# Opening of a fused attention and gated-MLP block: left-over Q/K rows on SyncE's queue, one more buffer for a transposed chunk, half of a chunk's statistics on ScalarE, long output columns first

## The chip, the cores and the metric

The kernel runs on one core of a Trainium2 chip. A core has five engines, each with its own instruction stream: TensorE (PE, matrix products; its weight loads are shown apart as PEld), VectorE (DVE), ScalarE (ACT), GpSimd (POOL) and SyncE (SP), which here only issues DMA transfers. Transfers are issued from the streams of SP, ACT and POOL and run on 16 DMA engines. The metric is the device time of one execution in microseconds; lower is better. Before the change it is 565.48 us (median of three runs, 563.97 to 566.1).

## What is computed

S = 2048 rows of D = 576 columns pass through an attention part (A) and a gated MLP part (B). Each is preceded by a layer norm, whose result is scaled and shifted by columns computed from a condition vector c, and followed by a gated residual. Attention has 32 heads of 18 columns and looks at 8 positions back, 2 apart. The MLP multiplies two projections to F = 4608 columns (no non-linear function) and projects back.

```
mod = (silu(c) @ w_mod)            # six rows of D: sa, ca, ga, sb, cb, gb
h = layernorm(x) * (1 + ca) + sa
q, k, v = split(h @ wqkv)          # 32 heads of 18
logits[s, w] = q[s] . k[s - 2 w] * 18 ** -0.5,  w = 0..7, masked where s - 2 w < 0
x = x + ga * (sum_w softmax(logits)[s, w] v[s - 2 w]) @ wo
h = layernorm(x) * (1 + cb) + sb
x = x + gb * ((h @ w_gate) * (h @ w_up)) @ w_down
```

All inputs and the output are bfloat16.

## The kernel before

The rows are cut into 8 chunks of 256 (`CH`), each of two halves of 128 (`ST` = 2, index j). D = 576 is handled as `KT` = 5 blocks of 128, the last with 64 rows only (kt = 4, the "left-over" rows of a weight). The order of the instructions of each engine is the order in which the program writes them; no scheduler moves them. What is emitted on one engine, or on one engine's DMA queue, runs in that order.

The program has an opening and then five groups of row tiles (`GROUPS`), each with a stage `gate_up` (36 steps f; 18 matmuls a step into the banks `pg` and `pu`, copies by ACT at L678 and L679, a product on DVE at L683) and a stage `down` (products with `w_down` into `acc` and `accr`). The attention of later chunks runs as pieces spread between the steps of these stages. The weight blocks `wgu` of `gate_up` (four steps each) come over SP's queue; in the first group blocks 0 to 4 are loaded ahead, and block 5 is issued when the matmuls of block 0 are done.

The opening handles chunk 0's attention whole, chunk 1's up to Q, K and V, and the same for chunk 2. Its loads go out in the order of the program: on SP's queue x of chunk 0, the blocks of `wmA` (the part of `w_mod` for sa and ca, kt = 0 to 3), the Q/K weights `wqk` for kt = 0, 1, then x of chunk 1 (`load_x(1)`), kt = 2, 3, then the value weights `wv`, x of chunk 2, `wmB`, `wo`, `wmC` (the ga part), and the first weights of the MLP. The left-over rows of `wqk` (kt = 4) are issued from ACT's stream, behind the third block of `wmA` (`behind(load_qk(nc.scalar, KF), wmA_in[2])`, L801).

The steps of the opening that the change and the prediction speak of:

- Columns of the modulation (`pm_part`, L824): matmuls with `wmA`, with idle matmuls (`run_idle`, L190) between the parts.
- Q and K of chunk 0 (`qk0`, L866): groups of nine matmuls, one group for each half j and each block kt, in the order (0, kt 0), (0, kt 1), (1, kt 0), (0, kt 4), (1, kt 1), (0, kt 2), (1, kt 4), (0, kt 3), (1, kt 2), (1, kt 3): `QKK` = (0, 1, 4, 2, 3). One of the nine reads `wq4`, columns of `wqk` that POOL copies together for each kt (L815). `qk0_out` copies the sums out of PSUM (L872 to L875).
- Logits of chunk 0: products on DVE (`pj`, L892), sums on PE (`lj`, L900), maximum and Exp (`max_j`, L906 to L908), sum and weights (`sum_j`, L914 to L916).
- Chunk i, i > 0: statistics (`a_ln`, L257 to L259: two BATCH_NORM_STATS2 and one aggregate for each half, on DVE), 1/sqrt by Ln and Exp on ACT (L262, L263), normalising on DVE (L267), transposes on PE and modulation into `hT` (`a_t`: L296, then L283 on DVE and L285 on ACT), Q and K (`a_q`, five calls, L374, copies by ACT at L377 to L382), V (`a_v`, L397 to L402). `hT` comes from the pool `hTp` with one buffer; chunk 0's comes from the pool `vshp` with two buffers, which otherwise holds the gathered values `vsh`.
- For chunk 2 the transposes of the two halves stand apart: `between` puts the second part of the ga row (`mod_row`, L321) and `to_keys` (L514, L517, copies L520) between them.
- `av_mul` (DVE, L529) and `av_sum` (PE, L540): values of chunk 0 times weights, and their sum; `b_wj` (L554): the product with `wo` for chunk 0.

In `down`, `b_o` transposes the attention output of a chunk (L502) and copies it to `oT` in two copies (L503: blocks 0 to 3 at once; L504: block 4); `b_w(i, j)` multiplies it with `wo`, first the last 64 columns (L569), then the first 512 (L571), and adds the residual on DVE (L573 to L575).

Of the kernel before, what the change touches and what calls it, by code (L numbers as in the profile page):

```python
# [7 lines left out]
BF = mybir.dt.bfloat16  # L8
F32 = mybir.dt.float32
# [9 lines left out]
P = 128  # L19
# [26 lines left out]
def kernel(  # L46
# [47 lines left out]
    def js(j):  # L94
        return slice(j * P, (j + 1) * P)
# [76 lines left out]
    def behind(dma, load):  # L172
        tc.add_manual_dep(dma.ins, load.ins.name, SYNC, reason="value rows go first")
# [13 lines left out]
    def run_idle(n):  # L187
        idle = ps([P, P], F32, "idle")
        for _ in range(n):
            nc.tensor.matmul(idle[:], lhsT=zero[:], rhs=zero[:], start=True, stop=True, skip_group_check=True)  # L190
# [23 lines left out]
    def load_wmA(eng, kt):  # L214
        p, r = rows(kt)
        return eng.dma_start(wmA[p, kt, :, :].rearrange("p b n -> p (b n)"), w_mod[r, 0:2 * D])

    def load_qk(eng, kt):
        p, r = rows(kt)
        return eng.dma_start(wqk[p, kt, :], A_wqkv[r, 0:2 * D])  # L220

    wmA_in = [load_wmA(nc.sync, kt) for kt in range(KF)]
    for kt in range(KF):
        if kt == 2:
            load_x(1)
        load_qk(nc.sync, kt)
# [22 lines left out]
    def ln_parts(src, tag):  # L249
        stats = small.tile([P, ST, 2, 6], F32, name="ln_stats" + tag)  # L250
        mv = small.tile([P, ST, 2], F32, name="ln_mv" + tag)
        rstd = small.tile([P, ST], F32, name="ln_rstd" + tag)
        xn = lnp.tile([P, ST, DP], BF, name="ln_xn")

        def stat(j, hfs=(0, 1)):
            for hf in hfs:
                nc.vector.bn_stats(stats[:, j, hf, :], src(j)[:, hf * 288:(hf + 1) * 288])  # L257
            if hfs[-1] == 1:
                nc.vector.bn_aggr(mv[:, j, :], stats[:, j, :, :].rearrange("p a b -> p (a b)"))  # L259

        def rsq(r):
            nc.scalar.activation(rstd[:, r], mv[:, r, 1], ACTF.Ln, bias=eps[:])  # L262
            nc.scalar.activation(rstd[:, r], rstd[:, r], ACTF.Exp, scale=-0.5)  # L263

        def norm(j):
            for d0, s0, n in ((0, 0, D), (D, D - 64, 64)):
                nc.vector.tensor_scalar(xn[:, j, d0:d0 + n], src(j)[:, s0:s0 + n], mv[:, j, 0:1], rstd[:, j:j + 1],  # L267
                                        ALU.subtract, ALU.mult)
        return xn, stat, rsq, norm

    def layernorm(src, tag):
        xn, stat, rsq, norm = ln_parts(src, tag)
        for j in range(ST):
            stat(j)

        def norms(js=range(ST)):
            for j in js:
                norm(j)
        return xn, lambda: rsq(slice(0, ST)), norms

    def modulate(dst, s, m, vi_scale, vi_shift, on_dve):
        if on_dve:
# [52 lines left out]
    def a_ln(i):  # L335
        x = x_in.pop(i)
        xn, rsq, norm = layernorm(lambda j: x[:, j, :], "a")
        aa[i] = dict(xn=xn, rsq=rsq, norm=norm)
# [3 lines left out]
        aa[i]["norm"]()  # L342

    def a_tiles(i):
        hT = hTp.tile([P, KT, CH], BF, name="hT") if i else vshp.tile([P, KT, CH], BF, name="vsh")
        aa[i].update(hT=hT, qT=qTs[i % 2], kT=kTs[i % 2])

    def a_halo(i):
# [6 lines left out]
    def a_t(i, on_dve=(0, 1, 2), between=None):  # L355
        a_tiles(i)
        hT = aa[i]["hT"]
        transposed(aa[i]["xn"], lambda m: hT[:, m, :], (0, 1), 0, between)(on_dve)
# [25 lines left out]
    def a_q(i, g):  # L384
        qk_tiles(i, QGRP[g], slice(0, CH), nc.scalar.copy)
        if g == 2:
            a_halo(i)
# [107 lines left out]
    def b_o(i):  # L495
        o = o_sbs[i % 2]
        pA = ps([P, 4, CH], BF, "oT_pA")
        pB = ps([P, 1, CH], BF, "oT_pB")
        for m in range(KT):
            d = pA[:, m, :] if m < 4 else pB[:, 0, :]  # L500
            for j in range(ST):
                nc.tensor.transpose(d[:, js(j)], o[:, j, m * P:(m + 1) * P], ident[:])  # L502
        nc.scalar.copy(oT[:, 0:4, :], pA[:])  # L503
        nc.scalar.copy(oT[:, 4, :], pB[:, 0, :])  # L504

    keyed = []
# [1 line left out]
    def to_keys(j):  # L508
        pk = ps([P, W, H], F32, "pk")
        for w in range(W):  # L510
            sh = DIL * (W - 1 - w)
            at = attn0[:, w // 4, :, w % 4, :]
            cross = j == 0 and sh > 0
            nc.tensor.matmul(pk[:, w, :], lhsT=slide[:, P + sh:2 * P + sh], rhs=at[:, j, :], start=True, stop=not cross,  # L514
                             skip_group_check=True)
            if cross:
                nc.tensor.matmul(pk[:, w, :], lhsT=slide[:, sh:P + sh], rhs=at[:, 1, :], start=False, stop=True,  # L517
                                 skip_group_check=True)
        kt = lgp.tile([P, W, H], BF, name="keyed", tag="lgs")
        nc.scalar.copy(kt[:], pk[:])  # L520
        keyed.append(kt)
# [43 lines left out]
    def b_w(i, j):  # L565
        pw = ps([P, 512], F32, "pw")
        pwr = ps([P, 64], F32, "pwr")
        for m in range(KT):
            nc.tensor.matmul(pwr[:], lhsT=oT[:, m, js(j)], rhs=wo[:, m, 512:D], start=(m == 0), stop=(m == KT - 1))  # L569
        for m in range(KT):  # L570
            nc.tensor.matmul(pw[:], lhsT=oT[:, m, js(j)], rhs=wo[:, m, 0:512], start=(m == 0), stop=(m == KT - 1))  # L571
        xt = x1p.tile([P, D], BF, name="x1")
        nc.vector.tensor_tensor(xt[:, 512:D], pwr[:], ga_bc[:, 512:D], ALU.mult)  # L573
        nc.vector.tensor_tensor(xt[:, 0:512], pw[:], ga_bc[:, 0:512], ALU.mult)
        nc.vector.tensor_tensor(xt[:], xt[:], x_res[i][:, j, :], ALU.add)  # L575
        x1.setdefault(i, []).append(xt)

# [220 lines left out]
    nc.vector.tensor_tensor(sc_w[:], wide(c_col), wide(e_f), ALU.mult)  # L798
    stat0(1)
    rsq0(slice(1, 2))  # L800
    behind(load_qk(nc.scalar, KF), wmA_in[2])  # L801
    for j in range(ST):
        norm0(j)
    nc.vector.tensor_copy(sc[:], sc_w[:, :, 0])
# [32 lines left out]
    t0(1)  # L837
    run_idle(2)
    pm_part(MODK[3])
    run_idle(8)  # L840
    pm_part(MODK[4])
    run_idle(5)

# [45 lines left out]
    def pj(j, w):  # L889
        off = HALO - DIL * (W - 1 - w) + j * P  # L890
        prods[j, w] = prodp.tile([P, KT, P], BF, name="prodj", tag="prod")
        nc.vector.tensor_tensor(prods[j, w][:], aa[0]["qT"][:, :, js(j)], aa[0]["kT"][:, :, off:off + P], ALU.mult)  # L892
# [53 lines left out]
        lj(0, w)  # L946
    for w in range(6, 8):
        pj(0, w)
    a_q(1, 0)
    for w in range(6, 8):  # L950
        lj(0, w)
# [12 lines left out]
    a_q(1, 3)  # L964
    for w in range(4, 6):
        lj(1, w)
    a_ln(2)
    aa[2]["rsq"]()
    a_q(1, 4)
    for w in range(6, 8):  # L970
        lj(1, w)
    max_j(1)
    mod_columns(wmB, 1)
    aa[2]["norm"]((0,))
    sum_j(1)
    aa[2]["norm"]((1,))
    a_v(1, 0)
    ga_row = lambda part: mod_row(lambda p, k: wmC[p, k, :] if k < KF else wmCr[p, :], ga_bc, sc_bc, (part,))
    ga_out = [ga_row((0, 512))]

    def between():
        ga_out.append(ga_row((512, D)))
        for j in range(ST):
            to_keys(j)

    a_t(2, (0, 1, 2), between)
    a_v(1, 1)
    av_mul(0, 0)
    av_mul(0, 1)
# [106 lines left out]
```

## Time and profile before

| | us |
|---|---|
| median of three runs (lowest, highest) | 565.48 (563.97, 566.1) |
| the profiled execution, time | 564.62 |
| its span, first to last instruction | 562.9 |
| PE busy in the span | 548.8 |
| DVE busy | 330.7 |
| ACT busy | 248.4 |
| start of the first `gate_up` matmul (L654) | 54.47 |
| start of the first product with `w_down` (L721) | 94.91 |

All times of single instructions are microseconds from the start of the span. A row of the timeline gives the start, the duration, the engine, the line, the operation, the tiles written and read with their shape, how many equal instructions are merged, and in brackets how long the engine stood idle before and what released it; a q behind the engine's name marks its instruction queue, which issues DMA transfers. A row of the windows view gives the stretch and its length, the busy time (and number of instructions) of PE, PEld, DVE, ACT and POOL, the granted clock of PE (1.00 is full speed), the mean busy share of the DMA engines, and GB/s.

Of the page, the costliest groups are the matmuls of the MLP:

```profile
L654 PE MATMUL pg<-h2T,wgu 64*128 64x512 bf16 (+2 forms) x1440 | 277.3, 333 | 0.0
L654 PE MATMUL pu<-h2T,wgu 64*128 64x512 bf16 (+2 forms) x1440 | 276.0, 333 | 0.0
...
L721 PE MATMUL acc<-wd,hh 128*128 128x512 bf16 (+1 forms) x556 | 140.2, 369 | 0.2
```

The columns behind the bar are the busy time, the mean duration in ns, and the idle time of the engine just before these instructions: the MLP's matmuls follow each other without a pause.

### The profile page before, as it was taken

The numbers are of one execution on the slowest core, as the hardware profiler recorded it, in microseconds if no ns is written. First come the engines' busy times: TensorE is split into PE (matmuls) and PEld (weight loads), VectorE is DVE, ScalarE is ACT, GpSimd is POOL, SyncE is SP. The second block draws the span as 40 slices with busy tenths as digits, with TensorE's granted clock in tenths as the row PEclk, the third lists the DMA queues.
The fourth block names the chain that finished last, engine by engine and source line by source line (L and its number), as shares of the span: only waits on it lengthen the run. The fifth ranks groups of instructions, "written<-read, shape, count | busy, mean of one in ns | idle before, by whom it ended". The sixth has DMA issues, their size and how long they took to land.

```text
span 562.9 us, 14324 instructions
## 1 busy us (share of the span) xinstructions
PE 548.8 (97%) x6021; PEld 328.1 (58%) x6059; DVE 330.7 (59%) x799; ACT 248.4 (44%) x572; POOL 66.8 (12%) x104
## 2 busy tenths in 40 slices
PE   6999999999999999999999999999999999999997
PEld 5777887666444445656444444665555555565564
DVE  7688889995767787251867787406727614322202
ACT  2545566244555653323355654231466611455500
POOL 5101301213000001111200100111100022000020
PEclk9899999999999999999999999999999999999999
DMA  8999999754844854332854765333856565655053
GB/s 276 263 269 262 322 295 355 246 168 116 297 137 163 281 156 141 94 108 89 280 172 148 227 211 169 108 106 125 300 189 201 188 201 170 191 181 196 1 170 115
DMA packets 69994, 108.14 MB, mean 192 GB/s; under 512 B 3658, under 2 KB 57754, under 8 KB 69930
## 3 DMA queue, kind: packets, MB, share of 16 engines
q1 hardware_dynamic: 58592, 61.13, 35.3%
q0 software_dynamic: 11168, 45.81, 25.4%
q8 instruction: 47, 0.77, 0.6%
q10 hardware_dynamic: 170, 0.30, 0.2%
q14 instruction: 17, 0.14, 0.1%
HBM read 102.78 MB, written 4.44 MB: 190 GB/s over the span
## 4 chain that ended last, share of the span: by engine, by line
PE 88%; DVE 1%; issue 1%; ACT 1%; ACTq 0%
PE pg L654 28%; PE pu L654 22%; PE acc L721 20%; PE pq L374 4%; PE accr L725 4%; PE pw L571 3%; PE pv L397 2%; PE lg L432 2%; PE tr_pA L296 1%; PE oT_pA L502 1%; PE tr_pB L296 1%; PE pwr L569 0%; DVE o_t L760 0%; PE lt L448 0%; PE pvr L399 0%
## 5 line engine op out<-in xcount | busy, mean ns | idle before, releaser
L654 PE MATMUL pg<-h2T,wgu 64*128 64x512 bf16 (+2 forms) x1440 | 277.3, 333 | 0.0
L654 PE MATMUL pu<-h2T,wgu 64*128 64x512 bf16 (+2 forms) x1440 | 276.0, 333 | 0.0
L654 PEld LDWEIGHTS <-wgu 64*128 64x128 bf16 x2880 | 141.3, 94 | 107.2 <-issue 0.5
L678 ACT CAST u_sb<-pu 128x512 bf16<-128x512 f32 (+2 forms) x180 | 90.1, 501 | 136.2 <-PE pg L654 134.6
L721 PE MATMUL acc<-wd,hh 128*128 128x512 bf16 (+1 forms) x556 | 140.2, 369 | 0.2
L683 DVE TENSOR_TENSOR hh<-g_sb,u_sb 128x512 bf16<-128x512 bf16 (+2 forms) x180 | 66.6, 372 | 99.3 <-ACT g_sb L679 97.8
L725 PE MATMUL accr<-wd,hh 128*128 128x64 bf16 x576 | 99.2, 193 | 1.5
L679 ACT CAST g_sb<-pg 128x512 bf16<-128x512 f32 (+2 forms) x180 | 91.4, 508 | 0.0
L721 PEld LDWEIGHTS <-hh 128*128 128x128 bf16 x588 | 55.3, 98 | 57.8 <-issue 1.7
L165 POOL DMA_DIRECT2D wd<-in_B_w_down_dram x45 | 33.8, 751 | 292.1 <-PE accr L725 239.8
L654 PE MATMUL pu<-h2T,wgr 64*128 64x512 bf16 (+2 forms) x180 | 60.2, 335 | 0.3 <-ACT u_sb L678 0.3
L654 PE MATMUL pg<-h2T,wgr 64*128 64x512 bf16 (+2 forms) x180 | 60.2, 335 | 0.2 <-DVE h2T L283 0.2
L725 PEld LDWEIGHTS <-hh 128*128 128x128 bf16 x576 | 51.7, 98 | 2.7 <-issue 0.2
L422 DVE TENSOR_TENSOR prod<-qT,kT 128x1280 bf16<-128x1280 bf16 x56 | 44.7, 816 | 2.6 <-PE lg L432 2.6
L482 DVE TENSOR_TENSOR vsh<-vsh,attn 128x1152 bf16<-128x1152 bf16 x56 | 40.9, 750 | 0.0
L374 PE MATMUL pq<-hT,wqk 128*128 128x256 bf16 x280 | 35.3, 273 | 0.6 <-DVE hT L283 0.5
L283 DVE TENSOR_SCALAR h2T<-tr_pA,modc 128x256 bf16<-128x256 bf16 (+1 forms) x27 | 8.8, 382 | 36.6 <-PE tr_pA L296 36.6
L374 PEld LDWEIGHTS <-wqk 128*128 128x128 bf16 x280 | 25.7, 98 | 5.8 <-DVE hT L283 0.6
L654 PEld LDWEIGHTS <-wgr 64*128 64x128 bf16 x360 | 18.0, 94 | 17.0 <-issue 4.5
L416 POOL DMA_DIRECT2D vsh<-vd x14 | 12.4, 890 | 123.6 <-DVE o_sb L493 84.4
L377 ACT CAST qT<-pq 128x512 bf16<-128x512 f32 x14 | 8.1, 581 | 28.4 <-PE pq L374 28.4
L489 DVE TENSOR_TENSOR vsh<-vsh 128x1152 bf16<-128x1152 bf16 x28 | 20.4, 750 | 0.0
(187 smaller groups left out, 482.3 us busy)
## 6 DMA issues: line engine op xcount, KB each, us to landing
wd<-in_B_w_down_dram POOLq DMA_DIRECT2D x45, 576.0 KB, 4.4
wgu<-in_B_w_gate_dram SPq DMA_DIRECT2D x45, 512.0 KB, 4.2
wgu<-in_B_w_up_dram SPq DMA_DIRECT2D x45, 512.0 KB, 5.7
vsh<-vd POOLq DMA_DIRECT2D x14, 1152.0 KB, 8.0
x_r<-in_A_x_dram SPq DMA_DIRECT2D x8, 288.0 KB, 7.1
out_dram<-x SPq DMA_DIRECT2D x15, 144.0 KB, 4.2
x_t<-in_A_x_dram SPq DMA_DIRECT2D x7, 288.0 KB, 4.9
vd<-v_sb POOLq DMA_DIRECT2D x14, 144.0 KB, 2.8
```

Source lines behind the costliest of these rows:

```text
L165: return nc.gpsimd.dma_start(wb[:], B_w_down[r0:r0 + FB * P, :].rearrange("(k p) n -> p k n", p=P))
L374: nc.tensor.matmul(pq[:, gi, :], lhsT=qk_w(kt, m), rhs=hT[:, kt, cols], start=(kt == 0), stop=(kt == KT - 1))
L422: nc.vector.tensor_tensor(prod[:], aa[i]["qT"][:], aa[i]["kT"][:, :, off:off + CH], ALU.mult)
L482: nc.vector.tensor_tensor(v, v, at, ALU.mult)
L489: nc.vector.tensor_tensor(vsh[:, d], vsh[:, d], vsh[:, 4 + 2 * s:6 + 2 * s], ALU.add)
L571: nc.tensor.matmul(pw[:], lhsT=oT[:, m, js(j)], rhs=wo[:, m, 0:512], start=(m == 0), stop=(m == KT - 1))
L654: return nc.tensor.matmul(bank[:, 0:N], lhsT=lhs, rhs=rhs, start=first, stop=last, skip_group_check=True)
L678: nc.scalar.copy(u[:, 0:N], pu[:, 0:N])
L679: nc.scalar.copy(g[:, 0:N], pg[:, 0:N])
L683: nc.vector.tensor_tensor(hh[:, f, 0:N], gu[0][:, 0:N], gu[1][:, 0:N], ALU.mult)
L721: nc.tensor.matmul(a[:], lhsT=hh[:, f, js(j)], rhs=wb[:, f % FB, cs], start=(f == 0), stop=(f == FT - 1))
L725: nc.tensor.matmul(accr[:, j, :], lhsT=hh[:, f, js(j)], rhs=wb[:, f % FB, 512:D], start=(f == 0 and j == 0), stop=(f == FT - 1), skip_grou ...
```

## The change

- The left-over rows of `wqk` are issued from SP's stream, third of the five blocks (the loop runs over `QKK`), ahead of `load_x(1)`; the load on ACT's stream and its dependency on `wmA` go.
- Chunk 1's `hT` comes from the pool `vshp`, as chunk 0's; chunk 2 is the first that uses `hTp`.
- Chunk 2's half 0: mean and variance are computed on ACT by four activations (`mean_var_on_act`: Identity with accumulated output for minus the mean, Square with accumulated output for the variance, Ln, Exp), emitted before `a_q(1, 0)`; they use the tile of the normalised half as scratch. Half 1 keeps its statistics on DVE (`stat_x2(1)`), now behind `a_q(1, 4)`. Normalising adds minus the mean and multiplies.
- The transposes of chunk 2's two halves stand together; the second part of the ga row and `to_keys` follow them.
- Five idle matmuls in place of eight ahead of the last part of `pm_part`.
- `b_o` copies blocks 0 to 3 in two copies of two blocks each. `b_w` computes the first 512 columns before the last 64 when j = 0, and the two products on DVE follow the same order; j = 1 is as before.

```diff
-    wmA_in = [load_wmA(nc.sync, kt) for kt in range(KF)]
     for kt in range(KF):
+        load_wmA(nc.sync, kt)
+    for kt in QKK:
         if kt == 2:
             load_x(1)
         load_qk(nc.sync, kt)
...
+    def mean_var_on_act(src, junk, minus_mean, rstd):
+        nc.scalar.activation(junk, src, ACTF.Identity, scale=-1.0 / D, accum_out=minus_mean)
+        nc.scalar.activation(junk, src, ACTF.Square, bias=minus_mean, accum_out=rstd)
+        nc.scalar.activation(rstd, rstd, ACTF.Ln, bias=eps[:], scale=1.0 / D)
+        nc.scalar.activation(rstd, rstd, ACTF.Exp, scale=-0.5)
...
     def a_tiles(i):
-        hT = hTp.tile([P, KT, CH], BF, name="hT") if i else vshp.tile([P, KT, CH], BF, name="vsh")
+        hT = hTp.tile([P, KT, CH], BF, name="hT") if i > 1 else vshp.tile([P, KT, CH], BF, name="vsh")
...
-        nc.scalar.copy(oT[:, 0:4, :], pA[:])
+        for m in (0, 2):
+            nc.scalar.copy(oT[:, m:m + 2, :], pA[:, m:m + 2, :])
         nc.scalar.copy(oT[:, 4, :], pB[:, 0, :])
...
-        for m in range(KT):
-            nc.tensor.matmul(pwr[:], lhsT=oT[:, m, js(j)], rhs=wo[:, m, 512:D], start=(m == 0), stop=(m == KT - 1))
-        for m in range(KT):
-            nc.tensor.matmul(pw[:], lhsT=oT[:, m, js(j)], rhs=wo[:, m, 0:512], start=(m == 0), stop=(m == KT - 1))
+        parts = [(pwr, slice(512, D)), (pw, slice(0, 512))]
+        if j == 0:
+            parts.reverse()
         xt = x1p.tile([P, D], BF, name="x1")
-        nc.vector.tensor_tensor(xt[:, 512:D], pwr[:], ga_bc[:, 512:D], ALU.mult)
-        nc.vector.tensor_tensor(xt[:, 0:512], pw[:], ga_bc[:, 0:512], ALU.mult)
+        for p_t, cs in parts:
+            for m in range(KT):
+                nc.tensor.matmul(p_t[:], lhsT=oT[:, m, js(j)], rhs=wo[:, m, cs], start=(m == 0), stop=(m == KT - 1))
+        for p_t, cs in parts:
+            nc.vector.tensor_tensor(xt[:, cs], p_t[:], ga_bc[:, cs], ALU.mult)
...
     rsq0(slice(1, 2))
-    behind(load_qk(nc.scalar, KF), wmA_in[2])
...
     pm_part(MODK[3])
-    run_idle(8)
+    run_idle(5)
     pm_part(MODK[4])
...
     for w in range(6, 8):
         pj(0, w)
+    x2 = x_in.pop(2)
+    xn_x2, stat_x2, rsq_x2, norm_x2 = ln_parts(lambda j: x2[:, j, :], "a")
+    aa[2] = dict(xn=xn_x2)
+    mean0, rstd0 = sp.tile([P, 1], F32, name="mean0"), sp.tile([P, 1], F32, name="rstd0")
+    mean_var_on_act(x2[:, 0, :], xn_x2[:, 0, 0:D], mean0[:], rstd0[:])
     a_q(1, 0)
...
-    a_ln(2)
-    aa[2]["rsq"]()
     a_q(1, 4)
+    stat_x2(1)
     for w in range(6, 8):
         lj(1, w)
     max_j(1)
     mod_columns(wmB, 1)
-    aa[2]["norm"]((0,))
+    rsq_x2(slice(1, 2))
+    for d0, s0, n in ((0, 0, D), (D, D - 64, 64)):
+        nc.vector.tensor_scalar(xn_x2[:, 0, d0:d0 + n], x2[:, 0, s0:s0 + n], mean0[:], rstd0[:], ALU.add, ALU.mult)
     sum_j(1)
-    aa[2]["norm"]((1,))
+    norm_x2(1)
     a_v(1, 0)
...
-    def between():
-        ga_out.append(ga_row((512, D)))
-        for j in range(ST):
-            to_keys(j)
-
-    a_t(2, (0, 1, 2), between)
+    a_t(2, (0, 1, 2))
+    ga_out.append(ga_row((512, D)))
+    for j in range(ST):
+        to_keys(j)
     a_v(1, 1)
```

## The prediction

> **What bounds the kernel now.** I read the page first: shares by engine, then the 40 slices, then the chain that ended last.
>
> ```profile
> PE 548.8 (97%) x6021; PEld 328.1 (58%) x6059; DVE 330.7 (59%) x799; ACT 248.4 (44%) x572; POOL 66.8 (12%) x104
> ...
> PEclk9899999999999999999999999999999999999999
> ...
> PE 88%; DVE 1%; issue 1%; ACT 1%; ACTq 0%
> ```
>
> TensorE (PE) is busy 97% of the span and makes 88% of the chain. A change that removes no matmul can therefore win only where PE stands still or runs below its clock, and the granted clock is low in one of the 40 slices only, the second. Nearly all idle time of PE lies in the opening, the first 54.5 us, so I read its timeline, the waits, and windows of half a microsecond.
>
> ```profile
> 8.06 0.47 ACTq L220 DMA_DIRECT2D wqk<-in_A_wqkv_dram  x1
> ...
> 14.55 0.77 PEld L866 LDWEIGHTS <-wqk 128*128 128x128 bf16 x8 [2.84 <-DMA wqk<-in_A_wqkv_dram]
> 14.56 1.04 PE L866 MATMUL pq<-vsh,wqk 128*128 128x128 bf16 x8 [2.67 <-DMA wqk<-in_A_wqkv_dram]
> ...
> 15.49 1.06 PE L866 MATMUL pq<-vsh,wqk 128*128 128x128 bf16 x8
> ...
> 18.08 0.39 PE L866 MATMUL pq<-vsh,wqk 128*128 128x128 bf16 x4
> ...
> 18.50 0.69 DVE L872 CAST kT<-pq 128x512 bf16<-128x512 f32 x1 [4.95 <-PE pq L866]
> ```
>
> The longest idle of PE in the run: 2.67 us, for a load of `wqk`. The 64 left-over rows (kt = 4) are third in PE's order QKK = (0, 1, 4, 2, 3); ScalarE (ACT) issues them at 8.06, and the view of DMA issues puts 6.5 us between that and landing: 14.5. VectorE (DVE) waits 4.95 us behind it. After the wait, matmuls of 128 columns take longer: eight take 1.06 us, later 0.6. The windows show why:
>
> ```profile
> 11.50:12.00 0.50, 0.39 (x8) 0.22 (x4) 0.50 (x3) 0.40 (x2) 0.00 (x0) 1.00 1.01 359
> ...
> 14.00:14.50 0.50, 0.00 (x0) 0.00 (x0) 0.00 (x0) 0.00 (x0) 0.00 (x0) 0.82 0.99 242
> 14.50:15.00 0.50, 0.44 (x5) 0.45 (x6) 0.00 (x0) 0.00 (x0) 0.44 (x2) 0.50 1.12 353
> ...
> 17.50:18.00 0.50, 0.50 (x10) 0.50 (x8) 0.00 (x0) 0.00 (x0) 0.00 (x0) 0.76 1.05 387
> ```
>
> The third column from the right is the granted clock: it falls to half at about 14.3 and returns at about 17.7. Two smaller idle places are touched as well:
>
> ```profile
> 37.41 1.05 DVE L283 TENSOR_SCALAR hT<-tr_pA,modc 128x256 bf16<-128x256 bf16 x3 [1.76 <-PE pvr L399]
> 37.88 1.67 PE L374 MATMUL pq<-hT,wqk 128*128 128x256 bf16 x10 [0.51 <-DVE hT L283]
> ...
> 39.78 2.68 PE L540 MATMUL po<-slide,vsh 128*128 128x142 bf16 x40 [0.23 <-DVE vsh L529]
> ...
> 97.54 1.01 ACT L503 COPY oT<-oT_pA 128x1024 bf16<-128x1024 bf16 x1 [0.38 <-PE oT_pA L502]
> 98.61 0.48 PE L569 MATMUL pwr<-wo,oT 128*128 128x64 bf16 x5 [0.50 <-ACT oT L503]
> ```
>
> Chunk 2's hT has one buffer with chunk 1's, so DVE and ACT wait until the last value matmul of chunk 1 (L399) has read it, and PE then waits for them. In the first down stage PE waits 0.50 us for one copy of 1024 columns.
>
> **A: the left-over rows on SP's queue.** One issue of about 0.45 us leaves ACT and joins SP's queue behind kt = 1 (issue 4.25 to 4.68), ahead of x of chunk 1, kt = 2, kt = 3 and the value weights wv. Those are issued some 0.5 us later, wv up to 1.6. Behind the queue that costs nothing: kt = 1 to 3 land 6.1, 8.1 and 8.9 us after issue (10.3, 13.4, 14.8), so they wait for bytes, not for the issue. The 147 KB take 0.4 to 0.6 us at the 240 to 390 GB/s of these windows, so kt = 4 should land at 10.7 to 11.2. PE wants it when it stops, at about 11.9: no wait. Then x of chunk 1 lands up to 0.5 late (DVE's statistics of it are not urgent), kt = 2 at 13.4 to 13.9, and kt = 3 still at about 14.8, since the same bytes come before it. PE runs (half 0, kt 4) and (half 1, kt 1), 0.46 each, until 12.8; waits about 0.8 for kt = 2; runs two groups until 14.5; waits 0.3 for kt = 3. The last group of half 0, which began at 18.08, begins at 14.86: 3.2 us earlier; 0.1 goes to POOL's copy into `wq4`, which now follows the landing directly. All of PE, DVE and ACT up to 20 hangs on this group. I take **3.1**.
>
> Bounds: kt = 3 0.5 earlier gives 3.6. If the clock halves as before, the group's first half costs 0.85 for 0.42, and kt = 3 0.4 later takes as much: 2.3. Before, the window from 11.9 to 14.3 had no matmul; now 1.8 us of it do work, so I take the full clock. *TensorE: Matmul & The Clock Gate* of the Trainium skill (Part 1) gives about 3.4 us to each window of the activity monitor, free-running, and an idle one for the drop. The stretch at half clock is 3.4 us long, in agreement, but the drop came with an idle time of only 2.67 us, so the measured row is the stricter one. By the page no gap left here would cost any clock and A stays 3.1; by the row alone the 1.8 us of work could be too little, and A would be 2.3.
>
> Who needs the later arrivals: the value matmuls (21.1 before, 18.0 after) want wv, landed at 16.6 and 17.1 before; the column sums of wmB (30.6, then 27.5) want it at 23.1; the ga row (33.1, then 30.0) wants its first block at 28.5. Least cover: 0.9 us.
>
> The five idle matmuls in place of eight ahead of the last wmA part (0.08 each, 8.62 to 9.07) save 0.15, but kt = 3 sets the time anyway: 0.
>
> **B: statistics and hT of chunk 2.** DVE loses one half's statistics (0.77 + 0.21 us). ACT gains four activations after its copy that ends at 25.04 and ahead of L377's copy of qT. No row shows an accumulating activation. Below: the copy of 256 columns takes 0.38 and of 1024 1.01, so 576 take 0.64. Above: L285, with two operands per partition, takes 0.45 for 128 and 0.56 for 256, so 0.85. With Ln 0.29 and Exp 0.20 the four are 1.8 to 2.2; I take 2.0. ACT was idle 0.74 there. L377 ends at 27.6 for 26.4, the Exp behind it 0.5 late, and sum_j(0) on DVE, which waits for that Exp, 0.3 late (27.77). ACT makes it up by L382, where it idled 0.35, and by the 2.1 us idle at 31.95. DVE's 0.3 comes off the 0.98 it saves.
>
> Then, in the clock of before: max_j(1) starts at 31.1 for 31.83; the columns of modc need PE until 32.05, so their chain (0.5), the norm (0.64), sum_j(1) (1.4) and the second norm (0.63) end at 35.2 for 35.65. Now the cost: PE's transposes of half 1, which stood behind to_keys, stand ahead of it and wait for this norm, from 34.45 to 35.25: 0.8 idle. In return the waits of 0.34 (attn, 35.16) and 0.51 (hT) go, and the slow stretch of 1.67 for a 1.25 group, because hT has its own buffer and is ready at 36.6, a microsecond before PE wants it. Transposes 0.3, ga part 0.24, keys 0.65, values 1.35: a_q(2, 0) from 37.75 to 39.0, and av_sum(0, 0) starts at 39.0 for 39.78 (its product on DVE is done at 38.3). I take **0.75**. Bounds: 0.2 if ACT's four take twice as long; 1.3 if the norm comes in time.
>
> **C: the down stage.** The copy becomes two of 512 columns, by the same rows 0.59 each; the first may start once its own transposes are done, 0.3 earlier, and ends at about 97.9. The long columns go first for j = 0, and PE stopped at 98.11: the wait of 0.50 goes, the second copy (98.5) is just in time for m = 2. The other six chunks show no wait at this line. **0.45**; bounds 0 and 0.6.
>
> Sum: 3.1 + 0.75 + 0.45 = 4.3 us. Behind 54.5 PE has no gap over 0.3 us except C's, so the shift goes through if the weights keep up (rival 3). The profiled execution took 564.62 (span 562.9 and 1.7 around it), so 560.3; the median is 565.48, so 561.2. I say 561.0.
>
> **Rivals.** 1: *the rows are late anyway.* The 64-row form, not the queue, is slow: wv's 64 rows took 8.3 us from issue to landing. But they stood behind two megabytes. If kt = 4 still landed at 14.5, A would be nothing: 564.3.
>
> 2: *the wait moves on.* kt = 2 and kt = 3 come later, since everything behind kt = 4 is pushed, and idle time in pieces still halves the clock. With kt = 3 at 15.4 and half clock to 18, A is 1.5: total 2.7, 562.8. For it: the transfers ran at only 212 to 258 GB/s from 12.5 to 14.5.
>
> 3: *the gain is handed back in the first gate/up stage.* Its block 5 is issued at 59.17, when block 0 is free, and its gate half lands 13.5 us later, at 72.7; the up half by about 74.5. PE reaches it at 76.87 before, 73.0 after: if it lands not a moment sooner, PE waits 1.5, total 2.8, 562.7. Against it: the issue itself comes 3.9 earlier, and the transfer engines were only 0.31 to 0.58 busy from 53 to 58, time that the values of chunk 1 on POOL's queue (issued 55.77) will now use.
>
> 4: *slower.* ACT's four activations hold up everything behind them in order: qT, the Exp, and with it DVE's sum_j(0), whose delay reaches PE one for one once ACT's cover (1.7) and DVE's 0.98 are spent. At 7 us for the four the whole gain is gone; at 10, 568.5. Reloads of the function table are the only way there that I see: the one load in the trace (L207) took 1.28 us, and three more would make 5.8. The changed program still has one load, so this is remote.
>
> **How the numbers follow.** Forecast 0.72, rivals 0.05, 0.10, 0.07, 0.06. A measurement of this kernel can tell about 0.5%, 2.8 us, from no change (the three runs span 2.1). The forecast's own spread, 2.5 to 5.6, is over that 95 times in 100; a fifth of rival 2 and a third of rival 3 are too: faster 0.68 + 0.02 + 0.02 = 0.72, slower 0.06, the rest 0.22. Range: the low end is the median less 5.6 and a microsecond of scatter, the high end takes in rivals 2 and 3: 558.9 to 564.4, with 1, most of 4 and the tails left out.
>
> **What would show it.** A: no wait of PE for kt = 4, waits under 1 us for kt = 2 and 3, clock 1.0 from 10 to 20, DVE's kT copy near 15.3; a wait over 2 us for any part of `wqk` refutes it. B: four ACT rows of about 2 us together near 21.9, transposes of half 1 waiting under 1 us for DVE, no wait for hT; av_sum near 36. C: no wait at the first of the long columns near 94. The first gate/up matmul starts near 50.6 for 54.47. If that holds and the end does not move, rival 3 is right.

## The result, and the profile after

| | before | after |
|---|---|---|
| median of all runs shown with the result (6 each) | 564.21 us (562.8 to 566.1) | 560.39 us (559.93 to 561.61) |
| ratio, 95% interval | | 0.9933 (0.991 to 0.9957) |
| the profiled execution, time (span) | 564.62 (562.9) | 561.61 (559.9) |

The change saves 3.8 us by the medians; 561.0 was forecast, with a saving of 4.3 counted from 565.48, the median of the first three runs of the kernel before; over its six runs that kernel is at 564.21. The profiled execution of the changed kernel is the slowest of its six, which matters below. The milestones of the two profiled executions, in us from the start of the span:

| | before | after | shift |
|---|---|---|---|
| first Q/K matmul of chunk 0 | 10.22 | 10.42 | +0.20 |
| DVE's first kT copy | 18.50 | 16.44 | -2.06 |
| first sum of logits (`lj`) | 20.16 | 18.10 | -2.06 |
| `av_sum` | 39.78 | 36.27 | -3.51 |
| first gate/up matmul | 54.47 | 50.92 | -3.55 |
| gate/up of the second group | 137.73 | 134.17 | -3.56 |
| last gate/up step of the fourth group | 446.93 | 443.38 | -3.55 |
| end | 562.89 | 559.91 | -2.98 |

So the opening gave 3.55, and the rest of the kernel kept it until the fourth `down` stage, where this execution lost 0.4 to a block of `w_down` that landed late, and 0.2 more behind it. Of the 3.55, the part up to `lj` gave 2.06 (A) and the part from `lj` to `av_sum` 1.45 (B); between the first and the second group, where C lies, nothing was gained.

From the page of the changed kernel, the shares by engine and the granted clock in 40 slices:

```profile
PE 550.0 (98%) x6056; PEld 327.3 (58%) x6056; DVE 330.4 (59%) x796; ACT 250.8 (45%) x585; POOL 66.9 (12%) x104
...
PEclk9999999999999999999999999999999999999999
```

PE is as busy as before in a span 3 us shorter, and the one slice with a low clock is gone. PE's timeline over the Q/K groups of chunk 0, and DVE's first copy:

```profile
11.32 0.62 PE L875 MATMUL pq<-vsh,wqk 128*128 128x128 bf16 x8 [0.24 <-DMA wqk<-in_A_wqkv_dram]
...
12.84 0.61 PE L875 MATMUL pq<-vsh,wqk 128*128 128x128 bf16 x8
13.29 0.22 PE L875 MATMUL pq<-vsh,wq 128*128 128x128 bf16 x1
15.00 0.62 PE L875 MATMUL pq<-vsh,wqk 128*128 128x128 bf16 x8 [1.49 <-DMA wqk<-in_A_wqkv_dram]
...
16.44 0.69 DVE L881 CAST kT<-pq 128x512 bf16<-128x512 f32 x1 [1.94 <-PE pq L875]
```

The group for kt 4 and the one behind it run without a break until 13.5. PE then waits 1.49 us for kt 2, which lands at 14.95, and kt 3 follows at 15.70; groups of eight keep their 0.61. In windows of half a microsecond (third column from the right: the granted clock):

```profile
11.50:12.00 0.50, 0.50 (x12) 0.50 (x10) 0.35 (x2) 0.50 (x2) 0.18 (x2) 1.00 1.03 369
14.00:14.50 0.50, 0.00 (x0) 0.00 (x0) 0.46 (x2) 0.00 (x0) 0.00 (x0) 1.00 1.14 323
15.00:15.50 0.50, 0.50 (x9) 0.50 (x10) 0.00 (x0) 0.00 (x0) 0.29 (x1) 1.00 1.09 307
```

The clock stays at full speed. Next, the statistics on ACT and the stretch to `av_sum`, from the timeline of all engines:

```profile
22.85 0.72 ACT L283 ACTIVATE ln_xn<-x_t 128x576 bf16<-128x576 bf16 x1
23.43 0.22 ACT L283 ACTIVATION_READ_ACCUMULATOR ln_xn<-x_t 128x1 f32 x1
23.69 0.78 ACT L284 ACTIVATE ln_xn<-x_t,mean 128x576 bf16<-128x576 bf16 x1
24.37 0.19 ACT L284 ACTIVATION_READ_ACCUMULATOR ln_xn<-x_t,mean 128x1 f32 x1
24.59 0.30 ACT L285 ACTIVATE rstd<-rstd,eps 128x1 f32<-128x1 f32 x1
24.92 0.20 ACT L286 ACTIVATE rstd<-rstd 128x1 f32<-128x1 f32 x1
...
32.94 0.34 PE L303 MATMUL tr_pA<-ident,ln_xn 128*128 128x128 bf16 x3 [0.36 <-DVE ln_xn L268]
...
35.17 1.26 PE L381 MATMUL pq<-hT,wqk 128*128 128x256 bf16 x10
```

The four activations are six rows and hold ACT for 2.2 us (22.85 to 25.03, where the next copy starts). PE waits 0.36 for the norm of half 1 and not at all for hT. Last, the first out projection of the `down` stage, with ACT's two copies:

```profile
93.99 1.07 ACT L511 COPY oT<-oT_pA 128x512 bf16<-128x512 bf16 x2 [0.38 <-PE oT_pA L509]
...
94.63 1.31 PE L582 MATMUL pw<-wo,oT 128*128 128x512 bf16 x5
...
97.24 0.34 PE L303 MATMUL tr_pA<-ident,ln_xn 128*128 128x128 bf16 x3 [0.18 <-DVE ln_xn L268]
```

The wait of 0.50 ahead of the out projection is gone, and 2.6 us later there is a wait that was not there before: the transposes of chunk 3 now come ahead of DVE's norm.

### The profile page after: what moved, and what is told of

The parts are those of the page before. It is cut to its first block, busy times and chain, and to the rows that moved or that the text cites. A ratio compares the mean times of both kernels' runs of the same rounds, so it can differ in the third digit from the quotient of the medians.

```text
span 559.9 us, 14365 instructions
## 1 busy us (share of the span) xinstructions
PE 550.0 (98%) x6056; PEld 327.3 (58%) x6056; DVE 330.4 (59%) x796; ACT 250.8 (45%) x585; POOL 66.9 (12%) x104
## 4 chain that ended last, share of the span: by engine, by line
PE 70%; issue 16%; DVE 2%; POOL 2%; DMA 1%; ACT 0%; POOLq 0%; ACTq 0%
PE pg L664 22%; PE pu L664 18%; PE acc L731 16%; PE pq L381 4%; PE accr L735 2%; PE pw L582 2%; PE pv L404 2%; PE lg L439 1%; POOL wd L165 1%; DMA wd<-in_B_w_down_dram 1%; PE tr_pA L303 1%; PE tr_pB L303 0%; DVE o_t L770 0%; PE oT_pA L509 0%; PE lt L455 0%
## 5 line engine op out<-in xcount | busy, mean ns | idle before, releaser
L731 PE MATMUL acc<-wd,hh 128*128 128x512 bf16 (+1 forms) x588 | 145.7, 370 | 0.3 <-DMA wd<-in_B_w_down_dram 0.2
L381 PE MATMUL pq<-hT,wqk 128*128 128x256 bf16 x240 | 30.0, 273 | 0.0
L584 DVE TENSOR_TENSOR x<-pw,ga_bc 128x512 bf16<-128x512 f32 x14 | 9.6, 688 | 22.3 <-PE pw L582 22.1
```

The lines of the kernel that those rows point to most:

```text
L381: nc.tensor.matmul(pq[:, gi, :], lhsT=qk_w(kt, m), rhs=hT[:, kt, cols], start=(kt == 0), stop=(kt == KT - 1))
L731: nc.tensor.matmul(a[:], lhsT=hh[:, f, js(j)], rhs=wb[:, f % FB, cs], start=(f == 0), stop=(f == FT - 1))
```

## Experiments

### Which transfer holds up kt 2: the bytes, or a fetch of instructions

In the changed kernel kt 2 landed 1.1 us later than the latest time forecast. The queue view of the window from 12.6 to 13.8 (packets, MB, share of the 16 DMA engines' time) has one packet that belongs to no load of the program:

```profile
q1 hardware_dynamic: 356, 0.43, 103.3%
q8 instruction: 1, 0.02, 5.7%
```

It is the next 16 KB of PE's instructions, and one DMA engine's share is 6.25%: the packet, recorded from 12.68 to 13.77, keeps one engine busy for 1.09 us. The loads' own queue (q1) fills the time of about all 16 engines in this window (103.3%), so its packets run on all of them side by side, and a load of `wqk` is complete when its last packet is. All packets of the size of a row of `wqk` (2304 bytes) that began before 13.4 had ended by 13.5; the next ones start only when the fetch has ended, and one behind the other: at 13.76, 14.00, 14.24, 14.48, 14.61 and 14.73, the last over at 14.89. That looks like one engine working off what was left for it, and is why the delay is longer than the fetch; the trace names no engine, so this last step is inferred. The page counts 47 such packets in the run, one for about 258 of PE's 12,112 instructions. To move the fetch without touching any load, the idle matmuls were made wider and fewer:

```diff
-        idle = ps([P, P], F32, "idle")
-        for _ in range(n):
-            nc.tensor.matmul(idle[:], lhsT=zero[:], rhs=zero[:], start=True, stop=True, skip_group_check=True)
+        idle = ps([P, 4, P], F32, "idle")
+        for k in [4] * (n // 4) + [n % 4] * (n % 4 > 0):
+            nc.tensor.matmul(idle[:, 0:k, :], lhsT=zero[:], rhs=zero[:, None, :].to_broadcast([P, k, P]),
+                             start=True, stop=True, skip_group_check=True)
```

> The changed kernel with PE's idle matmuls of the opening four times as wide and a quarter as many: the same busy time, about 58 matmuls and as many weight loads fewer ahead of Q/K. Theory: kt 2 and kt 3 land late (14.95 and 15.70 us) because a fetch of PE's next instructions, one packet of 16 KB from 12.68 to 13.77, holds one of the 16 DMA engines for 1.09 us. With about 116 instructions fewer before it, PE asks for that block later, after the Q/K groups have been fed: kt 2 lands at 13.4 to 14.0, PE waits 0.3 to 0.7 us for it instead of 1.49, DVE's first kT copy starts at 15.0 to 15.6 instead of 16.44, and the first gate/up matmul at 49.5 to 50.2 instead of 50.92: 558.9 to 559.7 us. Rival: the bytes in the queues set the landings. Then kt 2 and kt 3 land within 0.2 us of 14.95 and 15.70 wherever the fetch falls, PE waits 1.3 to 1.7 us, and the time stays at 560.4.

Measured: 559.93 us (559.45 to 560.24, 4 runs; ratio to before 0.9915, 0.989 to 0.9941). By the page's counts the edit takes out 43 matmuls and as many weight loads (6056 to 6013 each), not 58. The fetch falls at 14.66, kt 2 lands at 13.22 and kt 3 at 14.02, and PE's timeline has no wait for them:

```profile
12.74 0.61 PE L876 MATMUL pq<-vsh,wqk 128*128 128x128 bf16 x8
...
13.27 0.62 PE L876 MATMUL pq<-vsh,wqk 128*128 128x128 bf16 x8
...
14.71 0.69 DVE L882 CAST kT<-pq 128x512 bf16<-128x512 f32 x1 [0.24 <-PE pq L876]
```

The copy comes 1.73 us earlier than in the changed kernel. The theory had the direction, but 15.0 to 15.6 for the copy, 13.4 to 14.0 for kt 2 and 558.9 to 559.7 us for the time: the opening gained more than expected and the whole kernel less. But two of the other kernels of this job (below), with the changed kernel's own opening, also had kt 2 at 12.8 and 13.2, so one execution of each did not settle it. Three more kernels were run for it: the changed kernel twice more, the wide idle matmuls once more, and the opposite edit, in which every idle matmul is split into two of 64 columns:

```diff
-        for _ in range(n):
-            nc.tensor.matmul(idle[:], lhsT=zero[:], rhs=zero[:], start=True, stop=True, skip_group_check=True)
+        for k in range(2 * n):
+            cs = slice(64 * (k % 2), 64 * (k % 2) + 64)
+            nc.tensor.matmul(idle[:, cs], lhsT=zero[:], rhs=zero[:, cs], start=True, stop=True, skip_group_check=True)
```

> The changed kernel once more, for a second profiled execution beside those of the next kernels. Theory: the place at which the 16 KB fetch of PE's instructions falls among the loads of wqk differs from one execution to the next. PE's wait for kt 2 is then either about 1.5 us (kt 2 lands near 15.0, first kT copy 16.4) or under 0.3 us (kt 2 lands at 12.8 to 13.3, kt 3 at 14.4 to 14.7 with a wait of 0.2 to 0.6 us, first kT copy 15.1 to 15.3), and nothing in between; the median stays at 560.0 to 560.8, 0.3 to 0.9 us above that of the kernel with wide idle matmuls. Rival: the landings of the first profiled execution are the rule, then kt 2 lands at 14.8 to 15.1 again.

> The changed kernel as the control of the next two, on their chip. From the first Q/K matmul to the first lj matmul it took 7.6 to 7.8 us in three profiled executions (kt 2 caught by the fetch of PE's instructions) and 6.5 to 6.7 in three others (kernels with the same opening): one of these two again. Median 560.0 to 560.8.

> Wide idle matmuls again. Fetch theory: the stretch from the first Q/K matmul to the first lj matmul takes 5.9 to 6.1 us a third time, the fetch falls behind 14 us, and the median is 0.5 to 1.2 us below the control's, with a scatter between executions under the control's. Rival: as the control, within 0.3 us.

> The other direction: every idle matmul split in two of 64 columns, the same busy time, 78 matmuls and weight loads more ahead of Q/K or 156 instructions. The fetches move by so many instructions: the one that fell at 12.0 to 12.7 falls at 7 to 9.5 us, the next one at 15.5 to 18. Fetch theory: neither meets kt 2 or kt 3, so they land at 13.2 to 13.8 and 14.0 to 14.6, PE waits under 0.3 us for them, and the stretch from the first Q/K matmul to the first lj matmul takes 5.9 to 6.3 us, although there are more instructions and not fewer; an early fetch may delay wmA or kt 0 and so the first Q/K matmul by 0.3 to 1.0 us. Rival: it is the number of idle matmuls (or of weight loads) that matters and not where the fetch falls. Then the stretch takes 6.5 to 7.8 us as in the changed kernel, or more.

The changed kernel again: 560.58 (559.91 to 562.38) and 560.59 (559.52 to 561.53); wide idle matmuls again, on the chip of the second of these: 559.67 (559.0 to 560.49); narrow idle matmuls, there too: 560.12 (559.58 to 562.34). The first kT copies of the changed kernel came at 16.93 and 14.86, shifted from the places expected by the start of the Q/K groups (10.97 and 10.14 for 10.42). All profiled executions with kt 4 on SP's queue, the landings counted from that of kt 1, which itself moves between 10.67 and 11.69 from one execution to the next:

| kernel | fetch starts | kt 2 after kt 1 | kt 3 after kt 1 | first Q/K matmul to first `lj` |
|---|---|---|---|---|
| changed | 12.68 | 3.67 | 4.42 | 7.68 |
| changed, second time | 12.39 | 3.82 | 4.59 | 7.62 |
| statistics on DVE | 12.61 | 3.73 | 4.67 | 7.75 |
| changed, third time | 12.17 | 2.06 | 3.28 | 6.52 |
| old `down` | 12.01 | 2.00 | 3.66 | 6.70 |
| one buffer for hT | 12.14 | 2.03 | 3.45 | 6.51 |
| later transposes | 12.45 | 2.17 | 3.37 | 6.60 |
| wide idle | 14.66 | 2.04 | 2.84 | 5.97 |
| wide idle, second time | 14.44 | 2.10 | 2.88 | 5.60 |
| wide idle, later transposes | 15.40 | 2.10 | 2.94 | 6.01 |
| narrow idle | 8.38, 16.38 | 2.07 | 2.84 | 6.50 |

The four executions with no fetch between 10 and 14 us agree: kt 2 comes 2.04 to 2.10 us after kt 1, kt 3 2.84 to 2.94. The seven with a fetch at 12.0 to 12.7 fall into two groups: kt 2 is 1.6 us late and kt 3 with it, or kt 2 is in time and kt 3 0.4 to 0.8 us late. Nothing lies in between. That the narrow idle matmuls (60 matmuls and weight loads more) do the same to kt 2 and kt 3 as the wide ones (43 fewer) rules out their number and leaves where the fetch falls; there the expectation for the landings was met, and that for the stretch missed (6.50 for 5.9 to 6.3, at the edge of the rival's 6.5 to 7.8) because the first Q/K matmul came early (10.10) and PE waited 0.66 us for kt 1. Counted from the landing of kt 1, `lj` begins 5.22 us later there and 5.19 to 5.35 later with wide idle matmuls, against 5.57 to 5.93 and 6.82 to 6.96 in the two groups with a fetch at 12.0 to 12.7. The time of the narrow idle matmuls shows no gain all the same: three of their five executions took 559.6 to 560.1 us, the other two, with a mean granted clock of 0.997 and 0.995, 562.3 and 562.1. In the second execution with wide idle matmuls the stretch was 5.60, under the 5.9 expected, since kt 1 landed early there (10.67). Which of `wqk`'s loads a fetch at 12.0 to 12.7 meets is not a function of its start alone (12.39 meets kt 2, 12.45 does not); the trace doesn't say on which DMA engine a packet runs, so this stays open.

### Kt 4 on ACT's queue again

```diff
+    wmA_in = [load_wmA(nc.sync, kt) for kt in range(KF)]
     for kt in range(KF):
-        load_wmA(nc.sync, kt)
-    for kt in QKK:
...
     rsq0(slice(1, 2))
+    behind(load_qk(nc.scalar, KF), wmA_in[2])
```

> The changed kernel with the left-over rows (kt 4) back on ScalarE's queue, behind the last part of wmA that it issues. Theory: this queue place is what A is worth. kt 4 lands at 14 to 15 us again, PE waits 2 us or more for it, the granted clock falls to half from about 14.3 to 17.7, the first kT copy starts at 18.2 to 18.8, and the time is 2.1 to 3.3 us above the changed kernel's: 562.5 to 563.7. Rival: other parts of the change made the opening faster, then it is less than 1 us above.

Measured: 563.77 us (562.6 to 565.22, 10 runs), 3.2 above the changed kernel's 560.58 in the same job; by the means 3.1, give or take 1.0. That is A, by whole executions. The time is just past the 562.5 to 563.7 expected, and kt 4 landed later than 14 to 15, at 15.67; PE waited 3.14 us:

```profile
15.71 0.62 PE L875 MATMUL pq<-vsh,wqk 128*128 128x128 bf16 x8 [3.14 <-DMA wqk<-in_A_wqkv_dram]
...
16.23 0.61 PE L875 MATMUL pq<-vsh,wqk 128*128 128x128 bf16 x8
```

The kernel before, in the same job, took 564.23 us (17 runs; the ratio of this kernel to it is 0.999, 0.9974 to 1.0006). So with A undone the rest of the change shows 0.5 us by whole executions, where the traces show 1.45 for B in the opening; 1.45 stands at the edge of the interval, and no run shows what takes the difference.

The main point that was missed: the clock did not fall in the profiled execution, and the groups behind the wait take their usual 0.61. Hence a second profiled execution of the kernel before:

> The kernel before, a second profiled execution. In its first, PE idled 2.67 us for kt 4 and the clock fell to half; with the left-over rows back on ScalarE's queue PE idled 3.14 us and the clock did not fall. Theory: it hangs on where the idle time falls against a window that runs by itself, so either is possible here; kt 4 lands at 14 to 16 us and PE waits 2.4 to 3.4 us for it in both cases, and the stretch from the first Q/K matmul to the first lj matmul takes 9.6 to 10.2 us with the half clock and 8.6 to 9.2 without. Rival: the half clock belongs to this kernel, then it falls again.

It took 566.98 us (an execution of the same kernel beside it 564.79), PE waited 3.49 us for kt 4 (landed 15.84), and the clock fell again:

```profile
15.88 0.99 PE L866 MATMUL pq<-vsh,wqk 128*128 128x128 bf16 x8 [3.49 <-DMA wqk<-in_A_wqkv_dram]
...
16.78 1.06 PE L866 MATMUL pq<-vsh,wqk 128*128 128x128 bf16 x8
```

The stretch from the first Q/K matmul to `lj` took 10.89 us, above the 9.6 to 10.2 expected, since the wait was longer than forecast. With the half clock it was 9.94 and 10.89 in the two executions of before; without it, but with the same late rows, 8.92. Two of two falls against none of one would not decide between the theory and its rival; the mean granted clock of the other executions does. The stretch of 3.42 us at half clock in the trace lowers the mean of an execution of 563 us by 0.003. Of the 17 executions of the kernel before in the same job, 10 have a mean clock of 0.996 or 0.997 (565.1 us on average) and 7 one of 0.999 or 1.0 (563.6); of the 10 with the rows on ACT's queue, 5 have 0.994 to 0.997 (564.7) and 5 have 0.998 to 1.0 (563.2). All 18 of the changed kernel have 0.999 or 1.0. So the half clock belongs to neither kernel for good: with late rows it comes in about half of the executions, and those take 1.5 us longer.

The times at which the clock changes show what it hangs on. They are 4.08, 14.32 and 17.74 us in the first profiled execution of before and 5.72, 15.96 and 19.38 in the second: 10.24 and 3.42 apart in both, which is three steps and one step of 3.41, from a start of their own in each execution. In the step that ends with the fall, PE stood still for 2.4 us in the first (from 11.89) and for 3.3 in the second. In the execution with the rows on ACT's queue, steps counted from its first change (6.95) end at 10.36, 13.78 and 17.19; PE stood still from 12.57 to 15.71, 1.2 us in one step and 1.9 in the next, and the clock did not fall.

### What each part of B is worth

Chunk 1's hT back in the one buffer of chunk 2's, and, apart from it, both halves' statistics back on DVE (all of the opening's lines for them as before):

```diff
-        hT = hTp.tile([P, KT, CH], BF, name="hT") if i > 1 else vshp.tile([P, KT, CH], BF, name="vsh")
+        hT = hTp.tile([P, KT, CH], BF, name="hT") if i else vshp.tile([P, KT, CH], BF, name="vsh")
```

```diff
-    mean_var_on_act(x2[:, 0, :], xn_x2[:, 0, 0:D], mean0[:], rstd0[:])
...
+    a_ln(2)
+    aa[2]["rsq"]()
     a_q(1, 4)
-    stat_x2(1)
```

> The changed kernel with chunk 1's hT back in the one buffer that chunk 2's needs. Theory: most of the 1.45 us that B was worth comes from this buffer: DVE's evictions of hT wait again for the last value matmul of chunk 1, PE waits about 0.5 us for hT, and av_sum(0, 0) starts 1.0 to 1.6 us later, at 37.3 to 37.9 instead of 36.27. Rival: the buffer is worth little, since other work of PE fills the wait: av_sum(0, 0) at 36.2 to 36.6.

> The changed kernel with both halves of chunk 2's statistics on DVE and none on ScalarE. Theory: DVE's norm of half 1 comes 0.6 to 1.0 us later, PE's transposes of half 1 wait 0.9 to 1.4 us for it instead of 0.36, and av_sum(0, 0) starts at 36.8 to 37.2 instead of 36.27. Rival: with a buffer of its own for hT the order on DVE has slack, and av_sum(0, 0) starts at 36.2 to 36.5.

Their openings differ by the fetch, so they are read from `lj` to `av_sum`: 18.17 us in the changed kernel, 19.62 before, 20.01 with one buffer, 18.66 with the statistics on DVE. The buffer is worth 1.84 us, more than expected, and without it the rest of B costs 0.39; the statistics on ACT are worth 0.49, just under the expectation. With one buffer, PE's timeline:

```profile
33.85 0.33 PE L406 MATMUL pvr<-wv,hT 128*128 128x72 bf16 x5
35.28 1.25 PE L381 MATMUL pq<-hT,wqk 128*128 128x256 bf16 x10 [1.11 <-DVE hT L290]
```

PE finishes the last value matmul, which reads the old hT, and then stands for 1.11 us while DVE and ACT write the new one: with the transposes together no other work of PE is left to lie over it. Of the runs' own times (one each), 562.12 with one buffer is 1.8 above the changed kernel's execution with a like opening (560.36); 562.27 with the statistics on DVE lies between the changed kernel's two with a like opening (561.61 and 562.38) and shows nothing.

### C put back

The copy of `b_o` in one piece and the short columns first, as before.

> The changed kernel with the down part (C) as before: one copy of 1024 columns, short columns first. Theory: C moves a wait and saves nothing. PE waits 0.4 to 0.6 us again at the first matmul of the out projection near 94, the wait of 0.18 at the transposes at 97.24 is gone, and the gate/up matmuls of the second group of chunks start within 0.1 us of 134.17. Rival: C is worth its 0.45, then they start at 134.5 to 134.7.

Measured: 560.46 us in one run. From the first group's first gate/up matmul to the second group's: 83.26 us; in the changed kernel 83.25, before 83.26. C is worth 0.01. PE's timeline with the old `down`:

```profile
93.72 0.48 PE L576 MATMUL pwr<-wo,oT 128*128 128x64 bf16 x5 [0.50 <-ACT oT L510]
...
96.09 0.33 PE L303 MATMUL tr_pA<-ident,ln_xn 128*128 128x128 bf16 x3
```

The wait of 0.50 is back, and the transposes of chunk 3 don't wait. Step by step against the changed kernel, with their start in the first group lined up: the changed kernel is 0.53 ahead behind the out projection, 0.18 ahead behind the transposes of chunk 3, and level behind those of chunk 4. Both times PE arrives sooner and DVE's norm is no sooner. In the kernel before, the norm of chunk 3 on DVE and the transposes on PE already stood like this:

```profile
100.31 1.37 DVE L267 TENSOR_SCALAR ln_xn<-x_t,ln_mva,ln_rstda 128x576 bf16<-128x576 bf16 x4 [0.60 <-ACT ln_rstda L263]
```

```profile
100.98 0.33 PE L296 MATMUL tr_pA<-ident,ln_xn 128*128 128x128 bf16 x3
```

The first half's two of the four instructions end at about 101.0, and PE starts with them: no wait, and no slack.

To keep the gain, the transposes were put one step later, behind the second half of the out projection, with and without wide idle matmuls:

```diff
-        return ([lambda: a_ln(n), o[0], lambda: (a_norm(n), load_x(n + 2))] + [nop] * (3 if n == 4 else 0) + [o[1], lambda: a_t(n), o[2], o[3]] + q[:1] + [o[4]] + q[1:]
+        return ([lambda: a_ln(n), o[0], lambda: (a_norm(n), load_x(n + 2))] + [nop] * (3 if n == 4 else 0) + [o[1], o[2], lambda: a_t(n), o[3]] + q[:1] + [o[4]] + q[1:]
```

> Wide idle matmuls, and in the down stages the transposes of the next chunk one step later, behind the second half of the out projection. Theory: C's 0.50 us was given back at those transposes (0.34 for chunk 3, 0.16 for chunk 4), where PE overtook DVE's norm; one step of 1.1 us later the norm is done, both waits go, and the second group's gate/up starts 0.3 to 0.5 us earlier against the first group's than with wide idle matmuls alone. 559.1 to 559.6 us in the median. Rival: the wait moves on to DVE's evictions of hT ahead of the first Q/K matmuls (a_q), which now stand closer behind the transposes: gain under 0.15 us or a loss. In the opening, the fetch theory expects no wait over 0.3 us for kt 2 or kt 3 in this execution either, and the first kT copy at 14.6 to 15.0.

> The changed kernel with that later place of the transposes alone. Its down stage: as with wide idle matmuls, 0.3 to 0.5 us gained from the first to the second group's gate/up. Its opening is one more sample of the changed kernel's: by the fetch theory the first kT copy at 15.1 to 15.3 or at 16.4, later than 15.0 in either case.

Both lost: 561.87 us (560.76 to 562.83) and 562.3 (one run), and the stretch between the two groups grew to 85.33 in both, for 83.25 in the changed kernel and 83.41 and 83.73 with wide idle matmuls alone. PE's waits, wide idle matmuls:

```profile
100.38 0.38 PE L732 MATMUL acc<-wd,hh 128*128 128x512 bf16 x1 [1.05 <-DMA wd<-in_B_w_down_dram]
102.46 1.67 PE L382 MATMUL pq<-hT,wqk 128*128 128x256 bf16 x10 [0.44 <-DVE hT L291]
```

The rival was right, and more: hT isn't ready for the Q/K matmuls, PE also catches up with the weights of `down`, and the ten matmuls of Q/K take 1.67 us for 1.25. In the openings, the first kT copy came at 15.28 (wide idle, first Q/K matmul 0.5 later than usual) and 15.22.

### A version that beats both

Wide idle matmuls on top of the change: 559.93 and 559.67 us in two jobs, ratio to before 0.9917 (0.9896 to 0.9938) in the second. All its 10 runs against all 18 of the changed kernel: 0.9 us less in the mean, give or take 0.5. In its two profiled executions `lj` begins at 16.37 and 16.02, in the changed kernel's three at 18.10, 18.59 and 16.67; 0.2 and 0.5 us of it go again in the first `down` stage, where PE waits for a block of `w_down` (0.15 and 0.46).

## Why the prediction was right, and where not

**A, 3.1: right in the mean, by a path that held in part of the executions only.** Against its counterpart on one chip A is worth 3.1 or 3.2, give or take 1.0. No wait for kt 4, clock at 1.0, no wait over 2 us: as said. "kt = 2 at 13.4 to 13.9, and kt = 3 still at about 14.8" comes close where the fetch misses kt 2 (12.8 to 13.5 and 14.4 to 14.7 with the old `down`, with one buffer, with later transposes and in the third execution of the changed kernel), and their `lj` at 16.7 to 17.0 is 3.1 to 3.5 earlier than in the first execution of before. In the profiled execution the fetch met kt 2, the wait was 1.49 for the 0.8 forecast and the "under 1 us" of the signs, and A came to 2.06, below the lower bound of 2.3. The failed step is the sum of bytes: it took the transfers in SP's queue, at a rate, as all there was. Before, a fetch lay in the same place (11.14 to 12.23) and was not noticed; the lower bound allowed for the half clock and for kt 3 0.4 later, not for kt 2 a microsecond late.

That the mean agrees is in part luck. The forecast counted the half clock of the one trace of before as if it came in every execution. Against the changed kernel's 560.8, the executions with late rows and a mean clock of 0.998 or more are 2.3 longer, those below it 3.9; 3.1 is the mean of the two. So 3.1 is too high for executions without the fall and too low for those with it, in which the wait for kt 4 can also be longer than the 2.67 us of the trace that the forecast read (3.49 in the second execution).

The rule of the Trainium skill (*TensorE: Matmul & The Clock Gate*, Part 1), that the clock falls after an idle window of about 3.4 us whose start is its own, agrees with the steps of 3.41 us above, and with the changed kernel, where idle times of 1.49 and 1.63 us did not lower the clock. The window need not be wholly idle: 2.4 us of it were enough, and 1.9 were not.

**B, 0.75: mis-sized, 1.45.** The order of events was the forecast one; the rows were costed too long. ACT's four took 2.2 us for 2.0. Put into the clock of before (2.06 later), the transposes of half 1 began at 35.00 and not 35.25: they need the first of the norm's two instructions, not both. From them to `a_q` it took 2.23 us and not 2.5 (the ga part, the keys and the values were each costed by the whole duration of their rows, which overlap), and `a_q` to `av_sum` 1.10 for 1.25. These three are the 0.7 in the trace; whole executions leave open how much of the 1.45 lasts to the end, as said above. That B consists of the buffer, with the transposes together worth less than nothing without it, wasn't in the forecast.

**C, 0.45: wrong, 0.01.** "The wait of 0.50 goes": it did. The step that failed is the one behind it, "the shift goes through": PE had no wait behind this one in the trace of before, but no slack either at the transposes of chunk 3 and little at those of chunk 4. The wait moved from ACT's copy to DVE's norm.

**The rivals.** Rival 1 and rival 3 did not come: kt 4 was in time, and in the first gate/up stage block 5 was issued at 55.61 for 59.17, its gate half landed at 69.35 for 72.67, and the shift is -3.55 ahead of it and behind it. Rival 2 is half right: the wait did move on to kt 2, at full clock. Rival 4 did not come: 2.2 us for the four. In the profiled execution the terms erred in opposite directions, A by -1.04, B by +0.70 and C by -0.45 (2.06 + 1.45 + 0 = 3.51 for 4.3), so that the sum is nearer than its parts is luck too. Over all runs the parts do not add up: 3.1 or 3.2 and 1.45 are 4.6, and 3.4 to 3.8 was measured in three jobs. Part of that lies within the 1.0 of A; the rest is open. The five idle matmuls in place of eight were not tried apart: with the rows on ACT's queue and five of them, the first Q/K matmul began at 10.90, for 10.22 and 10.73 before, so no gain shows.

## What to carry to other kernels

Before forecasting a landing, list everything that moved in that window, not only the program's loads: a packet that holds one of 16 engines for a microsecond can delay a whole load that is spread over all of them. Behind a wait that is removed, look for the next consumer that only just did not wait; its slack bounds the gain. One profiled execution can be an unlucky one: where its time stands at the edge of the runs, read a second one before a cause is named, and read the granted clock of all executions before a stretch at half clock is counted in full.

## What was not expected of the hardware

A fetch of 16 KB of PE's instructions (1.09 us of one DMA engine) delayed the load of `wqk` behind it by 0.4 to 1.6 us in all seven executions in which it fell at 12.0 to 12.7 us, and 86 instructions fewer or 120 more in an unrelated place moved it away. *Runtime: NRT & Kernel Launch* of the Trainium skill (Instruction fetch mechanics) says that instructions come in blocks of 16 KiB, 256 instructions, by a queue of their own; the packets' size and their number (47 for 12,112) agree. It calls crossing a block mostly hidden; here the cost fell on a load of weights.

An activation with an accumulated output is two rows: 0.72 and 0.78 us for 576 columns, and a read of the accumulator of 0.22 and 0.19.
